# Transposes moved into the gaps of attention outputs, and one rounding moved behind a copy

## The chip, the cores and the metric

The kernel runs on one core of one Trainium2 chip. The core has TensorE (PE; its weight loads are shown apart as PEld), VectorE (DVE), ScalarE (ACT), GpSimd (POOL) and SyncE (SP, which here only issues DMAs). Each engine works through its own queue in the order in which the program was written; they meet at semaphores. The metric is the device time of one execution in microseconds (us).

## The reference

Retention (linear attention with decay, no softmax) feeds a two-layer network. B = 8 batches, H = 8 heads, S = 576 positions, 64 numbers per head; 4608 tokens in all, 512 numbers each; the hidden layer has 2048.

```python
scores = scale * np.matmul(q, k.transpose(0, 1, 3, 2))
gamma = 1.0 - 2.0 ** (-5.0 - np.arange(H, dtype=np.float32))
Dmat = np.where(rel >= 0, gamma[:, None, None] ** rel[None, :, :], 0.0)
ret = scores * Dmat[None, :, :, :]
out = np.matmul(ret, v)          # -> x: 4608 tokens x 512
h = x @ w_in
g = h * np.cos(h)
return (g @ w_out).astype(np.float32)
```

`rel` is the distance from a key's position to a query's.

## The kernel before, in words

**Tokens.** Attention goes by 18 blocks of 256 tokens, numbered from 0; the network goes by 9 tiles of 512 tokens, so tile n takes blocks 2n and 2n + 1. The decay is split into a factor on q and one on k, so that a masked product of chunks and a running state of 64 x 64 per head replace the full matrix: what a chunk gets from its own tokens goes through masked scores, and what it gets from earlier ones through the state, which is summed in float32 (`s_all`) and rounded to bf16 (`sb`).

**What a block goes through.** Its q, k, v are loaded by SP into `fq`, `fk`, `fv`. `scaled` (L192) multiplies q and k by the decay factors into `qks`, one instruction for each half (y = 0, 1) of q and of k, on POOL or DVE. `round_v` (L210) makes `vb`. `turned` (L225) transposes all of `qks` on TensorE with 32 small matmuls into PSUM, and two copies (`evacs`, L245) bring it to `qkT`; with two banks named, each copy has a bank of its own tag, and with one bank both halves lie in one PSUM tile. `scores` (L281) and `sums_of` (L347) are 32 and up to 32 small matmuls; DVE masks the scores into `ret` (L337) and adds the states (L406, L410), ACT rounds them (L420). `outputs` (L488) computes the block's result: `out_own` (L430) in two halves of 16 or 32 small matmuls, `out_carried` (L467) from the rounded states, and an ACT copy into the network's input x (L492).

**Between the halves of `out_own`.** The two halves write the same PSUM places from different rows of the array, so the second must wait until the first is complete. Without a guard, TensorE drains. With a guard, ACT makes a tiny copy (`flag`, L461) that waits for the first half, the second half waits for that copy, and the guard's instructions fill the time between: held-back ACT copies of outputs, and TensorE work such as the next block's states and scores.

```python
            if swap and guard is None:
                nc.tensor.drain()
            elif swap:
                gate = nc.scalar.copy(flag[:, 1:], flag[:, :1])
```

**The network.** `mm1` (L505) is the first matmul of one tile: 64 matmuls of 128 x 512 in 8 blocks (tiles 0 and 1 go in halves of 256 columns), in three PSUM buffers in turn; ACT takes the cosine and DVE multiplies (L530, L531). Work of the attention can be put inside it (`inside`, L950). `fillers` (L93) spreads a number of no-operations through a tile's `mm1`. The second matmul is direct for tile 0 (L1015, with an ordered list of steps, `todo`, put in between), and by `mm2_seven` (L648) with seven products of half size for tiles 1 to 8. It needs sums of blocks of g on DVE and POOL (L569) and sums of weights (L549). Between the products, `at` names which step of the attention goes where; results are copied by ACT (`held`, L660), added by DVE (L656, put off in `pend` until `flush`) and stored by SP. All the order is written out by hand.

**The places that matter here.** In tile 0's second matmul: block 2's outputs at step 58, the turn of block 3 at step 63, then the rounding of its v on ACT. In tile 1: after the last product but one, `last_outputs` (L1081) makes block 5's outputs. In tile 2: `mm1` has the turn of block 6 in its second block and that of block 7 in its sixth (L957, L958). Its products go in the order 1, 2, 6, 4, 7, 5, 3. Before product 2 comes `turning` (L1033) with block 8's turn; before 6 `only_intro` (L1048) with states and scores of block 6; before 7 `mid_unit` (L1085) with block 6's outputs, whose guard does the states and scores of block 7; before 3 `end_unit` (L1098) with block 7's outputs, whose guard does those of block 8. From tile 3 on the pattern is the same in each tile.

Of the kernel before, what the change touches and what calls it, by code (L numbers as in the profile page):

```python
# [17 lines left out]
def kernel(  # L18
# [9 lines left out]
    nc = tc.nc  # L28
# [4 lines left out]
    HP = P // 2  # L33
# [56 lines left out]
    w_in_sb = consts.tile([P, DG, DF], BF16)  # L90
    w_out_sb = consts.tile([P, ET, DM], BF16)

    fillers = {1: 80, 2: 76, 3: 126, 4: 48, 5: 64, 6: 64, 7: 128}  # L93
    tiles = {}

    class Chunk:
# [125 lines left out]
    def new_qkT(j):  # L222
        tiles["qkT", j] = nat.tile([P, 2, 2, HG, P], BF16, tag="qkT", name="qkT")

    def turned(j, banks, evacs=(nc.scalar.copy,) * 2):  # L225

        new_qkT(j)
        shape = [P, 2, 2, HG, HP]
        if len(banks) == 1:
            both = psum.tile([P, 2, *shape[1:]], BF16, tag=banks[0], name="tr")  # L230
            pss = [both[:, r] for r in range(2)]
        else:
            pss = [psum.tile(shape, BF16, tag=t, name="tr") for t in banks]
        for m in range(2):
            for y in range(2):
                for hg in range(HG):
                    for r in range(2):
                        rows = slice(r * HP, r * HP + HP)
                        nc.tensor.transpose(  # L239
                            pss[r][:, m, y, hg, :],  # L240
                            tiles["qks", j][rows, m, y, hg].rearrange("s a d -> s (a d)"),
                            ident[rows, rows],
                        )
        for r in range(2):
            evacs[r](tiles["qkT", j][:, :, :, :, r * HP : r * HP + HP], pss[r])  # L245

    def transpose_pe(j, name, bank, evac, ys=(0, 1)):
        if ("qkT", j) not in tiles:
# [181 lines left out]
    def out_own(j, ps, guard=None):  # L430

        ret = tiles["ret", j]
        vb = tiles["vb", j]
        begun = set()
        gate = None
        if chunks[j][0].pair:
            order = [(c, y) for c in chunks[j] for y in range(2)]
        else:
            order = [(c, c.y) for c in chunks[j]]
        for swap in (1, 0):  # L440
            for hg in range(0, HG, 2):
                for c, y in order:
                    he = c.half ^ swap
                    for h in (head(he, hg), head(he, hg + 1)):
                        part = (h % 2, he)
                        i = nc.tensor.matmul(  # L446
                            ov_cols(c, ps, h, c.n),
                            lhsT=vb[c.rows, y, h, :],
                            rhs=ret[c.rows, he, h % HG, y, :],
                            start=part not in begun,  # L450
                            stop=False,
                            skip_group_check=True,
                        )
                        if gate is not None:
                            after(i, gate)
                            gate = None
                        begun.add(part)
# [4 lines that stand above are left out]
                after(gate, i)  # L462
                while held:
                    held.pop(0)()
                guard()

    def out_carried(j, ps):  # L467
        cs = [c for c in chunks[j] if c.carry]
# [13 lines left out]
    def x_of(j):  # L482
        n = j // 2
        if ("x", n) not in tiles:
            tiles["x", n] = xp.tile([P, DG, W], BF16, tag="xT", name="xT")
        return tiles["x", n][:, :, j % 2 * BK : j % 2 * BK + BK]

    def outputs(j, bank, guard=None):  # L488
        ps = psum.tile([P, DG, BK], F32, tag=bank, name="ov")
        out_own(j, ps, guard)  # L490
        out_carried(j, ps)
        nc.scalar.copy(x_of(j), ps)  # L492

    def spread(n, w):

# [441 lines left out]
    def states_and_scores(j, st_bank, sc_bank):  # L937
# [4 lines left out]
        for masked in masks:  # L942
            masked()

    stores = []

    for n in range(NT):
        blocks = blocks_of.get(n) or [(e + k * E2, 0, W) for e in range(0, E2, 2) for k in range(2)]
        for i, (et, c0, cw) in enumerate(blocks):
            inside = {  # L950
                (0, 0): {2: block1_own, 3: block1_carried},
                (1, 0): {3: lambda: states_and_scores(3, None, ("n", "st"))},
                (1, 1): {3: lambda: adds.append(sums_of(3, ("n", "st"))())},
                (1, 2): {3: lambda: (adds.pop()(), w_sums(4, 4, E2))},
                (1, 4): {2: lambda: turned(4, ("st", "a"), (act, vec))},
                (1, 7): {2: lambda: turned(5, "m")},
                (2, 1): {1: lambda: turned(6, ("n", "st"))},  # L957
                (2, 5): {1: lambda: turned(7, ("n", "st"))},  # L958
            }.get((n, i), {})
            mm1(n, et, c0, cw, banks_of.get(n, turn_of(n) * 3)[i], inside)  # L960
            if (n, i) == (1, 0):
                step(False)
                load_next()
            if (n, i) == (1, 1):
                step(False)
                for r0, ot in stores[3:] + stores[:3]:
                    stored_rows(r0, 0, DM, ot)
                load_next()
                step()
            if (n, i) == (1, 3):  # L970
                w_sums(7, 0, 4)
                w_sums(7, 4, E2)
                mm2_seven(1, {}, None, (1,), lambda: outputs(3, "a"))
            if n:
                sums_after(n, i)
            if n == 2 and i in (2, 4):
                for y in range(2):
                    scaled(nc.gpsimd, 8, "q" if i == 2 else "k", y)
            if (n, i) == (2, 6):
                round_v(8)  # L980
                prepared = 9
                load_next()
                load_next()
        if n == 0:
# [6 lines left out]
                (36, lambda: turned(2, "ab", (act, vec))),  # L991
                (36, lambda: round_v(2)),
                (45, lambda: states_and_scores(2, "a", "b")),
                (46, lambda: prep(3, nc.vector)),
                (60, load_next),
                (63, lambda: turned(3, "ab", (act, vec))),
                (63, lambda: round_v(3, (act, act))),
                (58, lambda: outputs(2, "b")),
            ]
            todo += [  # L1000
                (at, lambda x=x, e=e: w_sums(x, e, e + 4))
# [29 lines left out]
        sc_bank, out_bank, st_bank = turn_of(n)  # L1031

        def turning(flush, pend):  # L1033
            for j, bank in ((b, st_bank), (b + 1, sc_bank)) if n > 2 else ((8, "m"),):
                if j < NB:
                    turned(j, bank)

        def first_unit(flush, pend):
            visit(b, sc_bank, st_bank, pend, flush, (a, out_bank))
# [7 lines left out]

        def only_intro(flush, pend):  # L1048
            flush()
            add = sums_of(a, "a")  # L1050
            for masked in scores(a, "m"):
                masked()
            add()()
# [25 lines left out]
            pass  # L1079

        def last_outputs(flush, pend):  # L1081
            outputs(b, "a")
            flush()

        def mid_unit(flush, pend):  # L1085
            masks, sums = [], []

            def middle():
                sums.append(sums_of(b, "b"))
                masks.extend(scores(b, "m"))  # L1090

            outputs(a, "a", middle)
            for masked in masks:
                masked()
            flush()
            sums[0]()()

        def end_unit(flush, pend):  # L1098
            visit(b + 1, "a", "b", pend, flush, (b, "m"))
# [47 lines left out]
```

## Time and profile before

| what | us |
|---|---|
| median of 3 runs | 294.38 |
| lowest, highest | 294.01, 295.45 |
| the profiled execution | 294.59 |
| its span, first to last instruction | 292.9 |

The profile is of one execution. Its span is divided among engines: a row of a timeline has the start, the time from the first start to the last end of what was merged into it, the engine, the line of the kernel, the operation, the tiles written and read, the count, and in brackets the idle time before it and what ended that. Ends of matmuls are modelled and overlap with what follows; starts, and above all the starts of weight loads, tell when TensorE came to something. A few matmul records can be missing.

### The profile page before, as it was taken

To read this page: it belongs to the slowest core of one execution; us is meant where nothing else is said; L and a number is where in the kernel's file an instruction comes from. 1 tells how busy PE (TensorE), PEld (TensorE's weight loads), DVE (VectorE), ACT (ScalarE), POOL (GpSimd) and SP (SyncE) were. 2 spreads that over 40 slices of the span, in tenths; PEclk is the share of its full clock that TensorE was granted. 3 is DMA by queue.
4 is the path that set the end of the run, shared out by engine and by line. 5 is a ranking of instruction groups with operands and counts; after the bars stand their busy time and mean duration, and the time that the engine had idled before them with its cause. 6 is when DMAs were issued, how large, how long until landed. Compare 5 with 4: busy or idle time off the path is not lost.

```text
span 292.9 us, 10506 instructions
## 1 busy us (share of the span) xinstructions
PE 283.8 (97%) x4365; PEld 195.7 (67%) x4385; DVE 218.6 (75%) x308; ACT 171.2 (58%) x201; POOL 143.4 (49%) x165
## 2 busy tenths in 40 slices
PE   8899999999999999999999999999999999999994
PEld 3578546888754786468746874688458845884584
DVE  5766747889948896897779776986698669745943
ACT  4766317756568745677476736673767476535620
POOL 7931353578595993369235933494248014101410
PEclk9999999999999999999999999999999999999999
DMA  7999999788997996915881489229201220112013
GB/s 226 263 184 204 249 243 249 188 202 214 236 243 200 258 257 167 223 32 119 208 214 41 101 208 222 50 63 249 58 0 40 55 57 0 40 47 64 0 38 107
DMA packets 103837, 42.62 MB, mean 146 GB/s; under 512 B 68464, under 2 KB 103280, under 8 KB 103792
## 3 DMA queue, kind: packets, MB, share of 16 engines
q1 hardware_dynamic: 99104, 37.37, 52.5%
q0 software_dynamic: 4240, 4.19, 8.9%
q8 instruction: 36, 0.59, 0.8%
q10 hardware_dynamic: 448, 0.39, 0.4%
q14 instruction: 9, 0.07, 0.1%
HBM read 36.70 MB, written 9.44 MB: 158 GB/s over the span
## 4 chain that ended last, share of the span: by engine, by line
PE 89%; DVE 6%; issue 2%; DMA 1%; ACT 1%; DVEq 0%
PE h L519 42%; PE o L630 31%; PE o L1015 5%; PE tr L239 3%; PE ov L446 3%; PE ov L473 2%; PE sc L328 2%; DVE ret L308 1%; DMA fk<-in_k_dram 1%; PE st L361 1%; DVE qks L171 1%; DVE gs L569 1%; DVE ret L337 1%; DVE s_all L410 1%; DVE gT L531 0%
## 5 line engine op out<-in xcount | busy, mean ns | idle before, releaser
L519 PE MATMUL h<-xT,w_in_sb 128*128 128x512 bf16 (+1 forms) x689 | 126.9, 340 | 1.0 <-issue 0.2
L531 DVE TENSOR_TENSOR gT<-h,cosh 128x1024 bf16<-128x1024 f32 x72 | 87.6, 1222 | 29.0 <-ACT cosh L530 28.7
L519 PEld LDWEIGHTS <-w_in_sb 128*128 128x128 bf16 x704 | 68.1, 98 | 54.6 <-issue 0.5
L530 ACT ACTIVATE cosh<-h,half_pi 128x1024 f32<-128x1024 f32 x72 | 79.8, 1114 | 39.5 <-PE h L519 39.4
L569 POOL TENSOR_TENSOR gs<-gT 128x512 bf16<-128x512 bf16 x28 | 35.8, 1278 | 99.6 <-DVE gT L531 99.6
L630 PEld LDWEIGHTS <-gs 128*128 128x128 bf16 x528 | 49.4, 98 | 6.3 <-DVE gs L569 0.4
L630 PEld LDWEIGHTS <-gT 128*128 128x128 bf16 x384 | 36.6, 98 | 6.1
L203 POOL TENSOR_TENSOR qks<-fk,gkc 128x512 bf16<-128x512 f32 x32 | 37.6, 1192 | 5.3 <-DMA fk<-in_k_dram 5.2
L656 DVE TENSOR_TENSOR ot<-ot,o 128x512 f32<-128x512 f32 x35 | 23.2, 683 | 21.5 <-ACT ot L660 14.2
L203 POOL TENSOR_TENSOR qks<-fq,gq 128x512 bf16<-128x512 f32 x29 | 32.6, 1144 | 12.5 <-DMA fq<-in_q_dram 12.5
L245 ACT COPY qkT<-tr 128x1024 bf16<-128x1024 bf16 x29 | 27.7, 1021 | 10.1 <-PE tr L239 10.1
L630 PE MATMUL o<-w_out_sb,gs 128*128 128x256 bf16 (+1 forms) x264 | 30.8, 270 | 0.1
L630 PE MATMUL o<-w_out_sb,gT 128*128 128x256 bf16 x256 | 30.6, 273 | 0.0
L630 PE MATMUL o<-ws,gs 128*128 128x256 bf16 (+1 forms) x264 | 30.5, 270 | 0.0
L660 ACT COPY ot<-o 128x512 f32<-128x512 f32 x33 | 19.2, 585 | 15.3 <-PE o L630 15.3
L420 ACT CAST sb<-s_all 128x768 bf16<-128x768 f32 (+2 forms) x17 | 15.7, 921 | 20.9 <-DVE s_all L410 17.8
L337 DVE TENSOR_TENSOR ret<-sc,mask_c 128x512 bf16<-128x512 f32 x32 | 20.6, 684 | 5.6 <-PE sc L328 4.5
L492 ACT CAST xT<-ov 128x1024 bf16<-128x1024 f32 x16 | 16.2, 1012 | 10.6 <-PE ov L473 10.5
L410 DVE TENSOR_TENSOR s_all<-st,s_all 128x256 f32<-128x256 f32 x49 | 20.7, 422 | 1.3
L214 POOL CAST vb<-fv 128x512 bf16<-128x512 f32 x33 | 20.5, 647 | 1.2 <-DMA fv<-in_v_dram 1.0
L569 DVE TENSOR_TENSOR gs<-gT 128x512 bf16<-128x512 bf16 (+1 forms) x25 | 17.5, 700 | 0.5
L630 PE MATMUL o<-ws,gT 128*128 128x256 bf16 x128 | 15.3, 273 | 0.0
(82 smaller groups left out, 212.7 us busy)
## 6 DMA issues: line engine op xcount, KB each, us to landing
out_dram<-ot SPq DMA_DIRECT2D x68, 128.0 KB, 2.5
fk<-in_k_dram SPq DMA_DIRECT2D x28, 256.0 KB, 5.1
fv<-in_v_dram SPq DMA_DIRECT2D x28, 256.0 KB, 4.9
fq<-in_q_dram SPq DMA_DIRECT2D x12, 512.0 KB, 5.0
w_out_sb<-in_moe_w_out_dram POOLq DMA_DIRECT2D x4, 512.0 KB, 10.1
w_in_sb<-in_moe_w_in_dram POOLq DMA_DIRECT2D x3, 512.0 KB, 8.5
fq<-in_q_dram SPq DMA_DIRECT2D x4, 384.0 KB, 5.8
fk<-in_k_dram SPq DMA_DIRECT2D x2, 512.0 KB, 4.9
```

The source lines that it names most:

```text
L203: return eng.tensor_tensor(out=dst.rearrange("p b a d -> p a b d"), in0=src.rearrange("p (a b) d -> p a b d", a=2), in1=by.rearrange("p (a ...
L214: runs[y](vb[:, y], f[:, :, y, :] if j < NP_B else f[:, y])
L245: evacs[r](tiles["qkT", j][:, :, :, :, r * HP : r * HP + HP], pss[r])
L337: nc.vector.tensor_tensor(out=ret[:, he].rearrange("p b y i -> p (b y) i"), in0=ps[he].rearrange("p b y i -> p (b y) i"), in1=mask_c.unsqu ...
L410: nc.vector.tensor_tensor(out=s32[:, u], in0=ps[c.half][:, c.y], in1=s32[:, u - 1] if u else tiles["run"], op=ALU.add,)
L519: nc.tensor.matmul(ps[:, j, :], lhsT=w_in_sb[:, dg, (et + j) * P : (et + j + 1) * P], rhs=xT[:, dg, c0 : c0 + w], start=dg == 0 and not (i ...
L530: nc.scalar.activation(cosh, ps, ACTF.Sin, bias=half_pi, scale=1.0)
L531: nc.vector.tensor_mul(gT[:, et : et + m, c0 : c0 + w], ps, cosh)
L569: i = eng.tensor_tensor(out=tiles["gs", n, x][:, e : e + step], in0=a[:, e : e + step], in1=b[:, e : e + step], op=op_,)
L630: nc.tensor.matmul(dst[i], lhsT=lhs[:, e, j * P : (j + 1) * P], rhs=rhs[:, e, c0:c1], start=(fresh and e == 0 and (i == 0 or len(parts) > 2)),
L656: return lambda: nc.vector.tensor_tensor(out=out_, in0=in0, in1=in1, op=ALU.add)
L660: held.append(lambda ps=tiles["all", x]: nc.scalar.copy(t, ps))
```

## The change

- Tile 0: the turn of block 3 becomes the guard of block 2's outputs, so that its drain is gone and a gate is there instead. The transposes of k come first (`ms=(1, 0)`), both halves lie in the one bank "a", and the two copies out (ACT and DVE) are issued after the copy of x (`later`). Of the scaling of block 3's q, one half goes to POOL (`prep3`); before, DVE did both.
- Tile 1: the turn of block 6 leaves tile 2's `mm1` and becomes the guard of block 5's outputs, in bank "m", copied out by ACT and DVE; this drain is gone too. The DVE copy is issued ahead of the additions of `flush`.
- Tile 2: the turn of block 7 leaves `mm1` and follows that of block 8 before product 2, in bank "a". Of each turn's two copies one goes to DVE; ACT did both of block 8's before. The states of block 6 go to bank "b" instead of "a".
- Tile 2: the rounding of block 7's states is put off from the end of `mid_unit` to the next `flush`, which comes behind product 7's output copy on ACT.
- Tile 2 has 80 fillers instead of 76.

```diff
-    fillers = {1: 80, 2: 76, 3: 126, 4: 48, 5: 64, 6: 64, 7: 128}
+    fillers = {1: 80, 2: 80, 3: 126, 4: 48, 5: 64, 6: 64, 7: 128}
...
-    def turned(j, banks, evacs=(nc.scalar.copy,) * 2):
+    def turned(j, banks, evacs=(nc.scalar.copy,) * 2, ms=(0, 1), later=False):
...
-        for m in range(2):
+        for m in ms:
...
-        for r in range(2):
-            evacs[r](tiles["qkT", j][:, :, :, :, r * HP : r * HP + HP], pss[r])
+        runs = [
+            lambda r=r: evacs[r](tiles["qkT", j][:, :, :, :, r * HP : r * HP + HP], pss[r])
+            for r in range(2)
+        ]
+        if later:
+            return runs
+        for run in runs:
+            run()
...
-                guard()
+                rest = guard()
+        return rest or ()
...
-        out_own(j, ps, guard)
+        rest = out_own(j, ps, guard)
         out_carried(j, ps)
         nc.scalar.copy(x_of(j), ps)
+        for run in rest:
+            run()
...
+    def prep3():
+        for name, y in (("k", 0), ("k", 1), ("q", 0)):
+            scaled(nc.gpsimd, 3, name, y)
+        scaled(nc.vector, 3, "q", 1)
...
-                (2, 1): {1: lambda: turned(6, ("n", "st"))},
-                (2, 5): {1: lambda: turned(7, ("n", "st"))},
...
-                (46, lambda: prep(3, nc.vector)),
+                (46, prep3),
                 (60, load_next),
-                (63, lambda: turned(3, "ab", (act, vec))),
+                (58, lambda: outputs(2, "b", lambda: turned(3, "a", (act, vec), (1, 0), True))),
                 (63, lambda: round_v(3, (act, act))),
-                (58, lambda: outputs(2, "b")),
...
-            for j, bank in ((b, st_bank), (b + 1, sc_bank)) if n > 2 else ((8, "m"),):
+            for j, bank in ((b, st_bank), (b + 1, sc_bank)) if n > 2 else ((8, "m"), (7, "a")):
                 if j < NB:
-                    turned(j, bank)
+                    turned(j, bank, (act, vec if n == 2 else act))
...
-            add = sums_of(a, "a")
+            add = sums_of(a, "b")
...
-            outputs(b, "a")
+            outputs(b, "a", lambda: turned(6, "m", (act, vec), later=True))
...
-            sums[0]()()
+            pend.append(sums[0]())
```

## The prediction

> **What bounds the kernel now.** I read the page's busy times first, then the chain of waits, then a table of two stages, then the timeline of each place that the diff touches, one engine at a time.
>
> ```profile
> PE 283.8 (97%) x4365; PEld 195.7 (67%) x4385; DVE 218.6 (75%) x308; ACT 171.2 (58%) x201; POOL 143.4 (49%) x165
> ```
>
> TensorE is busy nearly throughout, and the chain that ended last is PE for 89% and DVE for 6%. So time is won only where TensorE gets less to do or waits less, and lost where another engine comes late for it. Stage table of the first matmul of token tiles 2 and 3 (columns: stretch, length, busy time and count by engine, clock, DMA share, GB/s):
>
> ```profile
> 82.06:97.25 15.19, 14.93 (x127) 7.13 (x128) 9.75 (x10) 11.23 (x11) 11.24 (x12) 1.00 0.96 232
> 113.84:127.66 13.82, 13.71 (x65) 6.26 (x65) 11.39 (x15) 8.52 (x8) 3.85 (x3) 1.00 0.71 167
> ```
>
> Both hold the same 64 matmuls; tile 2 has two turns of 32 transposes inside. Its excess of 1.37 us is the price of two free-standing turns, 0.68 each. The clock is 1.00 in both.
>
> Weight loads at the outputs of block 5 (its halves parted by a drain) and of block 8 (a guard of 64 small matmuls between the halves):
>
> ```profile
> 79.37 0.21 PEld L446 LDWEIGHTS <-vb 64*64 64x64 bf16 x16 [0.43 <-DVE ret L337]
> 79.79 0.21 PEld L446 LDWEIGHTS <-vb 64*64 64x64 bf16 x16 [0.21 <-issue]
> ```
>
> ```profile
> 134.14 0.21 PEld L446 LDWEIGHTS <-vb 64*64 64x64 bf16 x16 [0.21 <-issue]
> 134.26 0.35 PEld L361 LDWEIGHTS <-qks 64*64 64x64 bf16 x32
> 134.53 0.36 PEld L328 LDWEIGHTS <-qkT 64*64 64x64 bf16 x32
> 134.80 0.36 PEld L446 LDWEIGHTS <-vb 64*64 64x64 bf16 x16
> ```
>
> From the first half to the second it is 0.42 with the drain and 0.66 with the guard. A half issues in 0.12 (134.14 to 134.26).
>
> The vector and scalar queues in the second matmul of tile 2, up to the gate of block 6's outputs:
>
> ```profile
> 98.60 1.22 DVE L531 TENSOR_TENSOR gT<-h,cosh 128x1024 bf16<-128x1024 f32 x1
> 99.86 0.68 DVE L569 TENSOR_TENSOR gs<-gT 128x512 bf16<-128x512 bf16 x1
> 100.57 0.98 DVE L569 TENSOR_TENSOR gs<-gs,gT 128x1024 bf16<-128x1024 bf16 x1
> 101.68 0.69 DVE L656 TENSOR_TENSOR ot<-ot,o 128x512 f32<-128x512 f32 x1
> 102.30 1.29 DVE L337 TENSOR_TENSOR ret<-sc,mask_c 128x512 bf16<-128x512 f32 x2
> 103.50 0.87 DVE L410 TENSOR_TENSOR s_all<-st,s_all 128x256 f32<-128x256 f32 x2
> 104.29 0.42 DVE L406 COPY s_all<-st 128x256 f32<-128x256 f32 x1
> ```
>
> ```profile
> 104.74 0.83 ACT L420 CAST sb<-s_all 128x768 bf16<-128x768 f32 x1 [3.04 <-DVE s_all L406]
> 105.48 0.58 ACT L660 COPY ot<-o 128x512 f32<-128x512 f32 x1
> 106.12 0.19 ACT L461 COPY flag<-flag 128x1 f32<-128x1 f32 x1
> ```
>
> DVE has no gap above 0.13 in this stretch; the rounding waits 3.04 for its last addition, the copy of an output and the gate (flag) stand behind the rounding in ACT's order, and the second half's loads start at 106.41. They are 0.67 behind the first half's (105.74), as in the undisturbed case above. So this chain and TensorE now arrive together: its slack is nil.
>
> The same queue at block 7's outputs, whose halves start at 110.50 and 111.54:
>
> ```profile
> 109.71 1.04 ACT L420 CAST sb<-s_all 128x1024 bf16<-128x1024 f32 x1 [1.53 <-DVE s_all L410]
> 110.66 0.58 ACT L660 COPY ot<-o 128x512 f32<-128x512 f32 x1
> 111.14 0.19 ACT L461 COPY flag<-flag 128x1 f32<-128x1 f32 x1
> ```
>
> Here the halves are 1.04 apart: the gate stands behind rounding and copy, and TensorE loses 1.04 - 0.66 = 0.38.
>
> **The change part by part.** One price first. Sixty-four transposes at 129.50 issue in 0.99, so 32 take 0.50; of a free-standing turn's 0.68 that leaves 0.18, or 0.09 for each change between large and small operands. As a guard, a turn makes the halves 0.12 + 0.09 + 0.50 + 0.09 = 0.80 apart, against 0.42 with the drain: +0.38. No row shows transposes between two halves. The low end is +0.24 (the gate's 0.66, if switching costs nothing); the high end takes each switch at the drain's 0.30 (0.42 - 0.12): 1.22, +0.80. I take 0.38, since the 0.09 comes from transposes.
>
> (a) Block 3's turn into block 2's outputs: -0.68 + 0.38 = -0.30 for TensorE. But the turn is moved before five 512-column matmuls, and its q rows are ready late. The outputs start at 45.68, the 16 k transposes end at 45.68 + 0.12 + 0.09 + 0.25 = 46.14. The q load is issued at 38.02 and takes 6.8 to land, 44.8. From there POOL scales one half and DVE (free from 45.09) the other. The pair like it:
>
> ```profile
> 37.58 1.55 POOL L203 TENSOR_TENSOR qks<-fq,gq 128x512 bf16<-128x512 f32 x1 [3.04 <-DMA fq<-in_q_dram]
> ```
>
> DVE ran its half beside it (37.53, 0.69), and both together took 1.60 instead of POOL's usual 1.04. So both halves are there at about 46.5 and TensorE waits 0.27 to 0.39, by which half is the late one; I take 0.33. The scalar queue then does x (from about 47.4), the turn's copy and the output's copy, 1.01 + 1.02 + 0.59 less some overlap, and frees bank n at about 49.95, where block 3's scores want it (49.95 now): 0.05. Sum for (a) +0.08; ends -0.30 (no wait) and +0.54 (dear switches and nothing else gained). Before, DVE finished q at 46.37 for transposes at 47.73, so there were 1.36 of cover; they are gone. POOL's added half falls into its idle time (44.55 to 49.62). The sums of weights on DVE slip by one copy of 0.69 and are not awaited before 49. SP's order of loads is unchanged.
>
> (b) Block 6's turn into block 5's outputs: +0.38 (0.24 to 0.80) there. Its q and k are ready by 70.5. DVE's copy now stands ahead of the closing additions at 79.34 and waits for the transposes until about 80.3, so the last of them ends near 84.5 instead of 82.95; SP reaches those stores only at 84.65 and DVE's next product is due at 85.25, so this is hidden, by 0.2 and 0.7.
>
> (c) Tile 2's first matmul loses both turns: -1.37. The ACT copies go with them; POOL's scaling of block 8 must be done 15.7 after the stage's start, and now ends 16.2 after it, paced in part by the same products, which come earlier; I count no wait, at most 0.3.
>
> (d) Blocks 8 and 7 turned together: 64 transposes take 129.50 to 130.54, 1.04, where 32 take 99.09 to 99.67, 0.58: +0.46.
>
> (e) Of their four copies two go to DVE, in front of the addition, masks and states of block 6: 2 x 0.69 = +1.38 in the chain shown above that has no slack. TensorE itself is 0.46 later, so the gate makes it wait 0.92. ACT keeps two copies, as now. Low end 0 (cover that I don't see), high end 1.38.
>
> (f) Block 7's rounding behind the copy: that copy waits only for a product that ends at 108.6, so it is done at about 109.4 to 110.0 and the gate no longer queues behind it; the rounding ends about 110.75 plus any shift, before the carried part needs it: -0.38, at worst 0. The additions on DVE that waited 1.60 for that copy come earlier, off the path.
>
> The four more fillers cost nothing that I can see: tile 3 has 126 in a stage without excess.
>
> Sum: 0.08 + 0.38 - 1.37 + 0.46 + 0.92 - 0.38 = +0.09 us. The profiled execution took 294.59 (span 292.9 and 1.7 around it), so it would be 294.68; the median shown is 294.38, 0.21 lower, and the forecast is 294.5.
>
> The Trainium skill, page TensorEngine Tiling, section Tiling Modes, Key Properties, says that changing the tiling mode, and not only the tile, drains TensorE. It speaks against (a) and (b), which put 64-row by 128-column work between 64 by 64 halves four times over; the 0.09 agrees with a cheap drain. With each switch as dear as the explicit drain the sum would be +0.93, which is the rival R2 below.
>
> **The rivals.**
>
> R1, the vector queue does not carry (e). Against it: the queue is dense and the gate is already just on time. For it: products and sums of tile 2 may come earlier than I shift them once ACT's turn copies are out of the first matmul. Then the sum is 0.09 - 0.92 = -0.83, or 293.6, and with no wait in (a) 293.2.
>
> R2, the other side, dear switches: (a) and (b) each 0.42 more, +0.93, 295.3. It decides from 0.10 a switch upward: each further 0.1 adds 0.4 over the four. For it: the 0.30 of the drain at 79.79; against it: 0.09 beside large matmuls.
>
> R3, block 3's q lands late: the cover of 1.36 is gone, so each us of lateness is one of TensorE's. Loads of these tiles in the stretch 25 to 60 take 4.5 to 8.2 by the medians of their groups; at 8.2 instead of 6.8 the sum is +1.5, 296.0. It decides from the first tenth; against it is that the order of loads is the same.
>
> R4, the reordered rounding does not help, because the gate still comes late: +0.47, 294.9.
>
> **How the numbers follow.** The forecast holds with 0.46 (with R4 inside it), 294.0 to 295.0; R1 0.25, R2 0.11, R3 0.08; 0.10 for what no row shows, shared by both sides. The range goes from R1's better case with a little scatter to R3: 293.1 to 296.0. A measurement of this kernel tells about 0.5%, 1.47 us, from no change. Below 292.9 only R1's better case with scatter and the unseen reach, 0.15; above 295.85, R3, the upper part of R2 and the unseen, 0.18; the rest, 0.67, is within.
>
> **What would show it.** Halves of blocks 2 and 5's outputs 0.8 apart, block 2's with a wait on qks in the middle; 13.8 in tile 2's first matmul; 1.0 for 64 transposes after its first product; two DVE copies of 0.69 ahead of L656, then block 6's halves 1.6 apart instead of 0.67; block 7's halves 0.66 apart. I am wrong if the gate at block 6 is on time (R1), if the halves are over 1 us apart without a wait on qks (R2), or if a later stage, which the change does not touch, has another length.

## The result, and the profile after

| | before | after |
|---|---|---|
| median, us (4 runs each) | 294.28 | 297.11 |
| lowest, highest | 294.01, 295.45 | 296.31, 299.94 |
| profiled execution | 294.59 | 299.94 |
| its span | 292.9 | 298.2 |
| mean granted clock in it | 1.000 | 0.992 |

The change makes the kernel slower: the ratio is 1.011, 95% interval 1.0084 to 1.0137. The profiled execution of after is the longest of its four; the other three took 297.07, 296.31 and 297.14 at a clock of 0.999 or more, so some of what this profile shows is its own, and it is told apart below. Ratios, here and below, leave out executions more than 1.5% above the shortest of the same kernel.

The totals on the page of after:

```profile
PE 285.6 (96%) x4366; PEld 197.5 (66%) x4385; DVE 218.9 (73%) x310; ACT 169.4 (57%) x200; POOL 144.6 (48%) x166
PEclk9999999799999999999999999999999999999999
```

TensorE is busy 1.8 longer than before, with the same work. One slice of the 40, the eighth (52.2 to 59.6), has a lower clock. So the place to look is tile 0's end, not tile 2, where I had most of my terms.

The span of after falls into these pieces (starts of the same weight loads in both traces):

| stretch of TensorE's work | before | after | difference |
|---|---|---|---|
| start to the first half of block 2's outputs | 45.68 | 45.83 | +0.15 |
| from there to the scores of block 3 | 4.27 | 7.73 | +3.46 |
| from there to block 4's turn | 10.29 | 11.82 | +1.53 |
| to block 5's outputs (first half) | 19.13 | 18.74 | -0.39 |
| block 5's outputs up to tile 2's first matmul | 2.69 | 3.09 | +0.40 |
| tile 2's first matmul | 15.19 | 13.81 | -1.38 |
| its second matmul | 16.59 | 18.15 | +1.56 |
| from tile 3 on | 179.06 | 179.03 | -0.03 |

All but 0.3 of the difference of 5.3 lies in the second and third row. The four rows of tiles 1 and 2 (the fourth to the seventh) sum to +0.19; my terms (b) to (f), which lie there, gave +0.01.

What happens in the second row, in the timeline of after (start, time, engine, line, operation, tiles, count, idle before it and what ended that):

```profile
45.83 0.21 PEld L452 LDWEIGHTS <-vb 64*64 64x64 bf16 x16 [0.42 <-issue]
46.08 0.29 PEld L239 LDWEIGHTS <-qks 64*128 64x128 bf16 x16
46.22 0.69 DVE L203 TENSOR_TENSOR qks<-fq,gq 128x512 bf16<-128x512 f32 x1 [0.90 <-DMA fq<-in_q_dram]
46.27 1.55 POOL L203 TENSOR_TENSOR qks<-fq,gq 128x512 bf16<-128x512 f32 x1 [1.24 <-DMA fq<-in_q_dram]
47.87 0.29 PEld L239 LDWEIGHTS <-qks 64*128 64x128 bf16 x16 [1.50 <-POOL qks L203]
48.21 0.21 PEld L452 LDWEIGHTS <-vb 64*64 64x64 bf16 x16
...
48.81 1.01 ACT L499 CAST xT<-ov 128x1024 bf16<-128x1024 f32 x1 [2.35 <-PE ov L480]
49.72 1.02 ACT L245 COPY qkT<-tr 128x1024 bf16<-128x1024 bf16 x1
50.77 0.69 DVE L245 COPY qkT<-tr 128x1024 bf16<-128x1024 bf16 x1 [3.25 <-ACT qkT L245]
51.36 0.11 PEld L334 LDWEIGHTS <-qkT 64*64 64x64 bf16 x2 [0.21 <-ACT ot L1036]
51.38 1.53 DVE L558 TENSOR_TENSOR ws<-w_out_sb,ws 128x1024 bf16<-128x1024 bf16 x1
52.84 0.68 DVE L1036 COPY ot<-o 128x512 f32<-128x512 f32 x1
53.56 0.44 PE L334 MATMUL sc<-qkT 64*64 64x64 bf16 x31 [1.99 <-DVE ot L1036]
```

There are two waits of TensorE here. The first is on q of block 3. Its load landed so late that DVE began its half at 46.22 and POOL at 46.27; POOL's took 1.55 beside DVE's and ended at 47.82, and the 16 transposes of q go at 47.87. The halves of the outputs are 2.38 apart (45.83 to 48.21), 1.58 more than the 0.80 that I took for a turn without a wait.

The second wait I had not seen at all. The DVE copy of the turn waits 3.25 for the ACT copy of the same turn, though it needs only transposes that were done at about 48.3. Both copies read one PSUM tile now, and they run one after the other. The ACT copy stands behind the cast of x in ACT's order, and the DVE copy behind the ACT copy; behind the DVE copy stand in DVE's order a sum of weights (1.53; before, it ran ahead of the copy, at 46.89) and the copy of tile 0's last output, and that output's PSUM bank is where the scores of block 3 want to go. TensorE comes to them at 51.36, and they start in earnest at 53.56: 2.20. Part of this is the sum: it took 1.53 here, where the part alone, below, has 0.68 for it, and that 0.85 is about the whole difference between 2.20 and the wait of 1.36 there.

The two waits and the guard's gain add up: -0.30 + 1.58 + 2.20 = 3.48, against 3.46 measured.

The third row of the table is the clock. Two stretches of the first matmul of tile 1 in after (columns: stretch, length, busy time and count of PE, PEld, DVE, ACT and POOL, granted clock, DMA share, GB/s):

```profile
54.00:57.00 3.00, 3.00 (x26) 2.00 (x28) 2.50 (x3) 1.11 (x1) 1.92 (x3) 0.59 1.00 252
57.00:60.00 3.00, 3.00 (x53) 2.61 (x54) 2.16 (x6) 1.59 (x2) 2.03 (x3) 0.84 0.95 214
```

PE is busy all the time, and the clock is 0.59 and then 0.84. That costs 3 x 0.41 + 3 x 0.16 = 1.7, about the 1.53 of the table, and it follows right on the two waits. The Trainium skill, page TensorE: Matmul & The Clock Gate, Part 1, says that the clock is halved after an idle window of some 3.4 us that runs by itself. The trace does not show that rule: neither wait is that long (1.58 and 2.20), and TensorE works for 3.5 between them (47.87 to 51.36). That the waits brought the clock down is not shown either. Executions with a mean clock of 0.994 came up in the kernel before (297.59), with tile 0's part undone (296.28) and with copies on ACT and no-operations moved (294.88), kernels whose profiles have neither wait; these three executions themselves were not profiled.

Tile 2, by the weight loads of after (the outputs of block 5 first):

```profile
84.12 0.21 PEld L452 LDWEIGHTS <-vb 64*64 64x64 bf16 x16 [0.35 <-DVE ret L343]
84.36 0.52 PEld L239 LDWEIGHTS <-qks 64*128 64x128 bf16 x32
84.94 0.21 PEld L452 LDWEIGHTS <-vb 64*64 64x64 bf16 x16
...
102.86 0.99 PEld L239 LDWEIGHTS <-qks 64*128 64x128 bf16 x64 [0.21 <-issue]
...
106.30 0.30 PEld L334 LDWEIGHTS <-qkT 64*64 64x64 bf16 x28 [0.21 <-issue]
107.59 0.11 PEld L334 LDWEIGHTS <-qkT 64*64 64x64 bf16 x3 [0.98 <-issue]
...
111.33 0.21 PEld L452 LDWEIGHTS <-vb 64*64 64x64 bf16 x16 [0.21 <-issue]
...
112.00 0.23 PEld L452 LDWEIGHTS <-vb 64*64 64x64 bf16 x16
...
116.22 0.21 PEld L452 LDWEIGHTS <-vb 64*64 64x64 bf16 x16 [0.21 <-DVE ot L665]
...
116.90 0.21 PEld L452 LDWEIGHTS <-vb 64*64 64x64 bf16 x16
```

Block 5's halves are 0.82 apart, block 6's 0.67 and block 7's 0.68. The wait that I had put at block 6's gate is not there. In its place stands a stop of about 1.0 in the middle of block 6's scores, between two loads of the same tile, that no engine ended ("issue").

### The profile page after: what moved, and what is told of

Its sections match the earlier page's. It is cut to its first block, busy times and chain, and to the rows that moved or that the text cites. A ratio compares the mean times of both kernels' runs of the same rounds, so it can differ in the third digit from the quotient of the medians.

```text
span 298.2 us, 10510 instructions
## 1 busy us (share of the span) xinstructions
PE 285.6 (96%) x4366; PEld 197.5 (66%) x4385; DVE 218.9 (73%) x310; ACT 169.4 (57%) x200; POOL 144.6 (48%) x166
## 4 chain that ended last, share of the span: by engine, by line
PE 72%; DMA 10%; DVE 7%; POOL 3%; SPq 2%; ACT 2%; issue 1%; POOLq 0%
PE h L528 34%; PE o L639 29%; DMA fq<-in_q_dram 5%; DMA w_in_sb<-in_moe_w_in_dram 3%; PE tr L239 2%; PE ov L452 2%; DVE gs L578 2%; DVE gT L540 2%; DMA fv<-in_v_dram 2%; SPq L140 2%; PE sc L334 1%; PE ov L480 1%; POOL qks L203 1%; ACT cosh L539 1%; PE st L367 1%
## 5 line engine op out<-in xcount | busy, mean ns | idle before, releaser
L528 PEld LDWEIGHTS <-w_in_sb 128*128 128x128 bf16 x704 | 68.9, 99 | 55.6 <-issue 0.3
L203 POOL TENSOR_TENSOR qks<-fq,gq 128x512 bf16<-128x512 f32 x30 | 35.1, 1189 | 9.3 <-DMA fq<-in_q_dram 8.6
L203 POOL TENSOR_TENSOR qks<-fk,gkc 128x512 bf16<-128x512 f32 x32 | 36.9, 1173 | 5.3 <-DMA fk<-in_k_dram 5.2
L245 ACT COPY qkT<-tr 128x1024 bf16<-128x1024 bf16 x26 | 24.9, 1023 | 9.5 <-PE tr L239 9.5
L214 POOL CAST vb<-fv 128x512 bf16<-128x512 f32 x33 | 19.9, 629 | 1.1 <-DMA fv<-in_v_dram 1.1
```

What stands on the lines that cost most here:

```text
L203: return eng.tensor_tensor(out=dst.rearrange("p b a d -> p a b d"), in0=src.rearrange("p (a b) d -> p a b d", a=2), in1=by.rearrange("p (a ...
L214: runs[y](vb[:, y], f[:, :, y, :] if j < NP_B else f[:, y])
L245: lambda r=r: evacs[r](tiles["qkT", j][:, :, :, :, r * HP : r * HP + HP], pss[r])
L528: nc.tensor.matmul(ps[:, j, :], lhsT=w_in_sb[:, dg, (et + j) * P : (et + j + 1) * P], rhs=xT[:, dg, c0 : c0 + w], start=dg == 0 and not (i ...
```

## The experiments

The theory after the result, call it T: the loss is all in (a), the block 3 edit, by the two waits; and the second wait comes from the one PSUM tile with two readers. Rivals: the loss is in tile 2 and only shows earlier; or it is the late q alone (R3 of the prediction); or it is the switches of tiling (R2). Inside tile 2 the question was what the stop in block 6's scores is: the DVE copies of (e), or something of TensorE's own. Before was run beside every group; where its median is given, it is that group's.

**Tile 0's part undone.** Tile 2 keeps all of the change.

```diff
-                (46, prep3),
+                (46, lambda: prep(3, nc.vector)),
-                (58, lambda: outputs(2, "b", lambda: turned(3, "a", (act, vec), (1, 0), True))),
+                (63, lambda: turned(3, "ab", (act, vec))),
+                (58, lambda: outputs(2, "b")),
-    fillers = {1: 80, 2: 80, ...
+    fillers = {1: 80, 2: 78, ...
```

> The changed kernel with tile 0's part undone (block 3's turn back at step 63 in banks a and b, block 2's outputs with their drain, both halves of q on DVE; 78 fillers in tile 2). Theory T (the loss is in tile 0: TensorE waits 1.57 us for block 3's q inside the guard and 2.2 us at block 3's scores): parts (b) to (f) are worth +0.2 us in the profile after, so this one takes 294.0 to 295.0 us and is the same as before within 0.3%; the scores of block 3 follow 1.4 us after the start of tile 1's first matmul. Rival S (the loss is in tiles 1 and 2, and the profiled execution's waits in tile 0 are its own): it stays above 296 us. Either way the wait of about 1.07 us inside block 6's scores stays.

Measured: 294.44 (293.63 to 296.28, 10 runs) against 294.54 before; ratio 1.0000, interval 0.9983 to 1.0018. The whole loss is gone. From block 2's outputs to block 3's scores it takes 4.26, as before. So T's place is right, and the rival that puts the loss in tile 2 is out, since (b) to (f) together are worth nothing that can be measured: +0.0 with an interval of 0.5 either way.

**Tile 0's part alone**, in the kernel before (with 78 fillers in tile 2).

```diff
-                (46, lambda: prep(3, nc.vector)),
+                (46, prep3),
-                (63, lambda: turned(3, "ab", (act, vec))),
+                (58, lambda: outputs(2, "b", lambda: turned(3, "a", (act, vec), (1, 0), True))),
-                (58, lambda: outputs(2, "b")),
```

> The kernel before with tile 0's part of the change alone (78 fillers in tile 2). Theory T: 296.3 to 297.5 us, and block 3's scores are held by 1.5 to 2.3 us behind DVE's copy of an output, which stands behind the turn's DVE copy, which waits for ACT's copy of the same PSUM tile. Rival S: 294.2 to 294.8 us.

Measured: 296.70 (296.02 to 298.17, 5 runs); ratio 1.0078, interval 1.0052 to 1.0104. In the timeline of this kernel:

```profile
48.12 1.02 ACT L245 COPY qkT<-tr 128x1024 bf16<-128x1024 bf16 x1
...
49.17 0.69 DVE L245 COPY qkT<-tr 128x1024 bf16<-128x1024 bf16 x1 [2.24 <-ACT qkT L245]
49.78 0.68 DVE L558 TENSOR_TENSOR ws<-w_out_sb,ws 128x1024 bf16<-128x1024 bf16 x1
...
51.12 0.44 PE L334 MATMUL sc<-qkT 64*64 64x64 bf16 x31 [1.14 <-DVE ot L1038]
```

In this execution, the shortest of the five, q came nearly in time: the halves are 45.65 and 46.61, 0.96 apart, a wait of 0.16. The second wait is there all the same, 1.36 (49.76 to 51.12). The stretch from outputs to scores takes 5.47, +1.20; the terms give -0.30 + 0.16 + 1.36 = 1.22. So the second wait does not need the first, and it is the one that is paid in both profiles with this part as the change has it.

**Both copies of block 3's turn on DVE**, in after.

```diff
-                (58, lambda: outputs(2, "b", lambda: turned(3, "a", (act, vec), (1, 0), True))),
+                (58, lambda: outputs(2, "b", lambda: turned(3, "a", (vec, vec), (1, 0), True))),
```

> The changed kernel with both copies of block 3's turn on DVE. Theory T1 (of tile 0's loss the larger part is the copies' order: the DVE copy waits for ACT's, ACT's stands behind the copy of x): DVE copies right after the transposes, the wait of 2.2 us at block 3's scores shrinks to 0.3 or less and the time falls by about 2 us, to 294.5 to 295.3. Rival Q (the late q carries it and the wait at the scores only follows from it): the wait at the scores shrinks little and the time stays at 296.3 or more.

Measured: median 295.24, spread from 293.61 to 299.77 in 10 runs; ratio 1.0003, interval 0.9981 to 1.0026. The two longest, 299.07 and 299.77, had mean clocks of 0.992 and 0.993; the other eight have a median of 294.87. In the timeline of one of the eight (297.02, clock 1.000):

```profile
48.43 0.41 PE L239 MATMUL tr<-ident,qks 64*128 64x64 bf16 x16 [1.76 <-POOL qks L203]
...
48.88 1.29 DVE L245 COPY qkT<-tr 128x1024 bf16<-128x1024 bf16 x2 [0.81 <-PE tr L239]
...
50.52 1.47 PE L528 MATMUL h<-xT,w_in_sb 128*128 128x256 bf16 x12
...
51.92 0.45 PE L334 MATMUL sc<-qkT 64*64 64x64 bf16 x32
```

The copies follow the transposes at once, and the scores follow the twelve matmuls with no wait: the second wait is gone. The first is 1.96 here (halves 46.01 and 48.77), and the stretch takes 5.91, +1.64; the terms give -0.30 + 1.96 = 1.66. So both waits are real, each without the other. By these medians the second carries most of the loss: without it the kernel takes 294.87 instead of 297.11, 2.2 of the 2.8 that the change costs.

No run set the landing of q by itself, but the profiles show that it changes without any edit near it. In the kernels whose tile 0 is that of before, or differs only after q is scaled, the first scaling of q on DVE starts at 45.06 to 45.28 in seven profiles, where DVE comes free, and at 45.68, 46.07, 46.12 and 46.34 in four, waiting for the load. One of the four in the timeline, of tile 0's part undone:

```profile
46.07 1.29 DVE L203 TENSOR_TENSOR qks<-fq,gq 128x512 bf16<-128x512 f32 x2 [0.75 <-DMA fq<-in_q_dram]
```

And of a kernel described below, which differs from it in its no-operations alone:

```profile
46.34 1.29 DVE L203 TENSOR_TENSOR qks<-fq,gq 128x512 bf16<-128x512 f32 x2 [0.81 <-DMA fq<-in_q_dram]
```

There the transposes of q come at about 47.9 and the lateness is hidden. Where the turn is a guard, DVE started its half at 45.06 (part alone), 46.22 (after) and 46.78 (both copies on DVE), and TensorE waited 0.16, 1.58 and 1.96. That this also makes the wide spread of the times is an inference.

**One bank for block 3's turn, nothing else**, in the kernel before.

```diff
-                (63, lambda: turned(3, "ab", (act, vec))),
+                (63, lambda: turned(3, "a", (act, vec))),
```

> The kernel before, with block 3's turn left at step 63 but in one bank (a) with one copy on ACT and one on DVE, as in the change. If two copies out of one PSUM tile go one after the other across the engines, DVE's starts at the end of ACT's, about 49.4 us instead of 48.45, the output's copy behind it ends near 50.8 and block 3's scores start 0.7 to 1.0 us later: 295.0 to 295.5 us. If the order of the copies does not matter, both start together and the time is that of before.

Measured: 295.42 (295.24 to 296.82, 10 runs) against 294.71; ratio 1.0020, interval 0.9990 to 1.0051, which by itself is not told from no change. Its timeline tells more:

```profile
48.37 1.01 ACT L245 COPY qkT<-tr 128x1024 bf16<-128x1024 bf16 x1 [0.21 <-PE tr L239]
49.42 0.69 DVE L245 COPY qkT<-tr 128x1024 bf16<-128x1024 bf16 x1 [0.80 <-ACT qkT L245]
50.02 0.68 DVE L1025 COPY ot<-o 128x512 f32<-128x512 f32 x1
...
50.76 0.44 PE L328 MATMUL sc<-qkT 64*64 64x64 bf16 x31 [0.65 <-DVE ot L1025]
```

In the kernel before, with two banks, the two copies run side by side:

```profile
48.41 1.01 ACT L245 COPY qkT<-tr 128x1024 bf16<-128x1024 bf16 x1 [0.21 <-PE tr L239]
48.45 0.69 DVE L245 COPY qkT<-tr 128x1024 bf16<-128x1024 bf16 x1 [0.88 <-PE tr L239]
```

With one bank DVE's starts when ACT's is done. The scores start 5.12 after block 2's outputs instead of 4.27: +0.85. So sharing a bank is enough to put the copies in order, and through DVE's queue it reaches TensorE. What it costs in the change is more, because there the ACT copy itself stands behind the cast of x. No run gave the guard's turn two banks, so what the change would take with them is not shown.

With these, the stretch from block 2's outputs to block 3's scores, and the same terms for each kernel (the guard's -0.30 only where the turn is a guard):

| kernel | stretch | over before | wait on q | wait at the scores | sum of terms |
|---|---|---|---|---|---|
| before | 4.27 | | | | |
| tile 0's part undone | 4.26 | -0.01 | 0 | 0 | 0 |
| one bank only | 5.12 | +0.85 | 0 | 0.87 | 0.87 |
| both copies on DVE | 5.91 | +1.64 | 1.96 | 0 | 1.66 |
| tile 0's part alone | 5.47 | +1.20 | 0.16 | 1.36 | 1.22 |
| after | 7.73 | +3.46 | 1.58 | 2.20 | 3.48 |

From the scores to block 4's turn it is 10.28 or 10.29 in all but after, where the clock fell.

**The stop in tile 2.** In the profile of the kernel with tile 0's part undone, the stop is again in block 6's scores, 0.61 long:

```profile
102.13 0.11 PEld L334 LDWEIGHTS <-qkT 64*64 64x64 bf16 x2 [0.50 <-issue]
```

The next four kernels start from that one and ask whether it hangs on the DVE copies of turns 8 and 7, or on the place in TensorE's instruction stream. Forty of tile 3's no-operations moved into tile 2's first matmul shift that place and take nothing else away.

Only the no-operations moved:

```diff
-    fillers = {1: 80, 2: 78, 3: 126, ...
+    fillers = {1: 80, 2: 118, 3: 86, ...
```

> The kernel a_undone with 40 of tile 3's fillers moved to tile 2 and nothing else. Theory F (the stop inside block 6's scores is TensorE's instruction stream reaching a new block too early): the stop is gone, and the DVE copies, no longer covered by it, hold the gate of block 6: its halves 1.1 to 1.3 us apart instead of 0.67. Theory D alone (the DVE copies cause the stop): the stop of 0.6 to 1.1 us stays where it is.

Measured: 294.72 (293.54 to 296.15, 10 runs) against 294.71; ratio 0.9997, interval 0.9968 to 1.0025. Its weight loads:

```profile
105.99 0.21 PEld L452 LDWEIGHTS <-vb 64*64 64x64 bf16 x16 [0.21 <-issue]
...
107.19 0.14 PEld L334 LDWEIGHTS <-qkT 64*64 64x64 bf16 x6 [0.49 <-issue]
107.23 0.23 PEld L452 LDWEIGHTS <-vb 64*64 64x64 bf16 x16
```

The stop has left block 6's scores and now stands in block 7's, inside block 6's guard. That fits a place in the stream, and not block 6's scores or what they wait for; but each is one profile, and the stops turn out below to come and go. The halves of block 6 are 1.24 apart, and the gate (106.73) was late as well, so the second half would have waited even without the stop.

Both copies of turns 8 and 7 on ACT instead of one each on DVE, no-operations not moved:

```diff
-                    turned(j, bank, (act, vec if n == 2 else act))
+                    turned(j, bank, (act, act))
```

> The kernel a_undone with both copies of blocks 8 and 7's turns on ACT and the fillers left. Theory D: the stop inside block 6's scores goes, the time from the start of tile 2's second matmul to that of tile 3's first falls from 17.67 to about 16.8 us. Theory F: a stop of 0.5 to 1.1 us stays in the last scores of block 6, at the same instruction, ending 2.4 us after an instruction transfer starts, and the stretch stays at 17.4 us or more.

Measured: 294.45 (293.66 to 295.91, 10 runs) against 294.71; ratio 0.9989, interval 0.9960 to 1.0018. Both edits:

> The kernel a_undone with both copies of blocks 8 and 7's turns on ACT and 40 of tile 3's fillers moved to tile 2 (118 and 86). It takes away both suspected causes of the 1.4 us that tile 2's second matmul still loses: the two DVE copies (theory D), and the place at which TensorE's instruction stream passes from one 16 KB block to the next (theory F: in the profiles the unexplained stops of TensorE, in before at block 7's outputs and in after at block 6's scores, lie exactly 512 instructions apart and both end 2.4 to 2.5 us after an instruction transfer began). Both expect the 1.07 us wait inside block 6's scores to be gone and the gate of block 6 on time, 293.0 to 293.7 us; if neither is the cause it stays, and the time equals a_undone's.

Measured: 294.22 (293.35 to 295.92, 10 runs) against 294.54; ratio 0.9991, interval 0.9974 to 1.0009.

The second matmul of tile 2 in four kernels (columns as above): before, tile 0's part undone, and copies on ACT.

```profile
97.25:113.84 16.59, 16.37 (x441) 14.07 (x440) 14.52 (x23) 9.25 (x13) 15.27 (x17) 1.00 0.97 237
```

```profile
96.03:113.70 17.67, 17.18 (x474) 14.74 (x473) 16.47 (x27) 9.46 (x13) 15.75 (x17) 1.00 0.95 227
```

```profile
95.94:112.60 16.66, 16.66 (x474) 14.47 (x473) 15.54 (x24) 11.30 (x15) 15.76 (x17) 1.00 0.96 232
```

With the copies on DVE this stage is 17.67 long, with both on ACT 16.66; with both edits it is 16.76 (95.85 to 112.61). In the last two profiles no stop is to be seen. The 1.0 in these single profiles does not come back in the medians, 294.44 against 294.45 and 294.22.

The rounding of block 7's states put back ahead of the copy, with both other edits:

```diff
-            pend.append(sums[0]())
+            sums[0]()()
```

> The kernel u_actact_shift with the rounding of block 7's states back in its old place. If the rounding in front of the copy held the gate (the reading on record), block 7's halves are 0.9 to 1.05 us apart instead of 0.67, the time is 0.25 to 0.4 us longer. If the stop of 0.41 us in the kernel before was the instruction stream alone, the halves stay at 0.67 to 0.75 us.

Measured: 294.04 (293.31 to 295.06, 10 runs) against 294.71; ratio 0.9975, interval 0.9950 to 0.9999. Leaving (f) out does not make it slower; if anything the other way. Its weight loads at block 7's outputs:

```profile
109.94 0.21 PEld L452 LDWEIGHTS <-vb 64*64 64x64 bf16 x16 [0.21 <-issue]
...
110.82 0.21 PEld L452 LDWEIGHTS <-vb 64*64 64x64 bf16 x16
```

0.88 apart, against 0.68 in after: the gate is late again, by 0.2.

The version with copies on ACT and no-operations moved, once more with more runs, as the likeliest to beat before:

> The kernel u_actact_shift once more, timed longer: the changed kernel without tile 0's part, both copies of both turns on ACT, 40 fillers moved from tile 3 to tile 2. By its profile tile 2 is 1.2 us shorter than before; if the time follows, 293.0 to 293.8 us and a ratio of 0.995 to 0.998; if the time is taken back elsewhere, 294.0 to 294.6.

Measured: 294.07 (293.37 to 296.08, 12 runs) against 294.58 (17 runs); ratio 0.9992, interval 0.9972 to 1.0011. The nearest to a gain is the kernel with the rounding put back, whose interval ends at 0.9999; no version was clearly shown to beat the kernel before.

**Three kernels profiled again**, to see whether the stop stays where it was.

> The kernel a_undone, a second execution to look at. If the stop inside block 6's scores hangs on when the instruction transfer gets through, its length differs from 0.61 us and it again ends 2.4 us after the start of that transfer, or is absent where the transfer starts under 1.5 us after the last passing of a block; if it is set by the DVE copies it has 0.6 us again and ends with a DVE instruction. The gate of block 6 is late by the DVE copies only as far as the stop has not covered them.

> The kernel u_actact, a second execution. Its first had no stop, and its instruction transfer had started 0.96 us after the last passing of a block. If that was chance, a stop of up to 1 us may appear here at the same instruction; if the DVE copies are the cause, there is none, and block 6's halves are 0.67 apart again.

> The kernel before, a second execution. If the 0.41 us stop at block 7's outputs was the gate behind rounding and copy, the halves are 0.85 to 1.05 us apart again; the part of it that the instruction stream made can be absent, and then the halves are 0.85 to 0.9 apart, as in u_round.

Measured: 294.72, 294.59 and 294.36. Weight loads of the first of them, tile 0's part undone:

```profile
105.84 0.21 PEld L452 LDWEIGHTS <-vb 64*64 64x64 bf16 x16 [0.21 <-issue]
...
106.81 0.21 PEld L452 LDWEIGHTS <-vb 64*64 64x64 bf16 x16 [0.22 <-ACT flag L467]
```

Now there is no stop in block 6's scores, and block 6's gate is late, as the prediction had it: the halves are 0.97 apart, 0.3 over the 0.67 of an undisturbed gate. In the second, with copies on ACT, there are stops where its first profile had none:

```profile
101.91 0.11 PEld L334 LDWEIGHTS <-qkT 64*64 64x64 bf16 x2 [0.47 <-issue]
...
106.73 0.11 PEld L452 LDWEIGHTS <-vb 64*64 64x64 bf16 x2 [0.20 <-issue]
```

And in the third, the kernel before:

```profile
110.33 0.21 PEld L446 LDWEIGHTS <-vb 64*64 64x64 bf16 x16 [0.21 <-issue]
...
111.21 0.21 PEld L446 LDWEIGHTS <-vb 64*64 64x64 bf16 x16 [0.17 <-ACT flag L461]
```

Block 7's halves are 0.88 apart here, where the first profile of before had 1.04. That first profile has, between the two halves, the row

```profile
111.53 0.11 PEld L328 LDWEIGHTS <-qkT 64*64 64x64 bf16 x2 [0.33 <-issue]
```

which the second does not have: a stop of the same kind, in the kernel before too. So these stops come and go between executions of one kernel, and one profile cannot price an edit to better than about 1 us here.

## Why the prediction was wrong

The forecast was 294.5, within 0.5%; measured is 297.11, beyond the range's high end of 296.0. The step that failed is (a), "Sum for (a) +0.08; ends -0.30 (no wait) and +0.54": the stretch cost +3.46 in the profile, and the executions of the part alone ran about 2.2 over before.

- **The late q (in (a)).** I took a wait of 0.33, from a load of 6.8 and a landing at 44.8. It came some 1.4 later in after's profile, where the load was issued 0.5 later (38.52 for 38.02) and took about 7.7, and the wait was 1.58. The mechanism was in the prediction, as R3: "the cover of 1.36 is gone, so each us of lateness is one of TensorE's". What was wrong is its size and its chance. The step put a single load time of before into a place where TensorE now waits for it, and gave a chance of 0.08 to the case that it was late (at 296.0, where a load of 8.2 makes its sum 295.9), with "the order of loads is the same" against it. The order was the same and the time was not: q was late in four of eleven profiles where it costs nothing, and in two of three where it does.
- **The scores of block 3 (in (a)).** I gave 0.05, by following ACT's queue and bank n. I wrote that the sums of weights on DVE "slip by one copy of 0.69 and are not awaited before 49", and did not ask when that copy could start. It could start only after ACT's copy, because both now read one PSUM tile; that moved the whole DVE queue, with it the copy of the last output, and with that the bank for the scores: 2.20 in after (0.85 of it the longer sum), 1.36 in the part alone, 0.87 from the one bank by itself. The diff shows it ("ab" to "a"), and the description of the change says that both halves lie in one bank; I treated the bank as a name and not as an order.
- **The clock** was 1.00 in all that I read, and I had no term for it. In after's profile it took 1.53. No other profile here shows it, and its cause is open.
- **(b)** held in time: halves of block 5 0.82 apart, predicted 0.80. It missed the same order of copies as (a): out of the one tile of block 6's turn, DVE's copy waited 3.50 for ACT's and started at 87.57 in after. The closing additions behind it ended at 90.91, 6.8 after block 5's outputs, where I had 5.1 (84.5 less 79.37). That is more than the room of 0.2 and 0.7 that I had counted, and yet TensorE waited for none of it, with tile 2's first matmul at 13.81: there the forecast had luck. The 0.82 also settles R2: a switch costs about 0.1 there, not 0.30, and 32 transposes between two 64 by 64 halves ran at the pace of the free-standing ones.
- **(c)** held: 13.81 for tile 2's first matmul, predicted 13.8; -1.38 against -1.37.
- **(d)** held: 64 transposes from 102.86 take 1.04 to the next work (103.90), predicted 1.04.
- **(e)** had the right mechanism with too large a size, and was not always what ended the wait. By starts of matmuls, from the stage's start to block 6's second half it took 9.18 in before (97.25 to 106.43), 10.23 in the second profile of tile 0's part undone (96.59 to 106.82) and 9.64 with the copies on ACT. Against before that is +0.46 with the copies on ACT, which is (d) to the digit, and +1.05 with two of them on DVE; so the copies cost 0.59, where I had 0.92. DVE's queue is as dense as I read it: the rounding behind it starts 8.77 into the stage instead of 7.49, later by what the two copies take one after the other (1.27 from 101.13, where I had 1.38). But the gate starts only 1.11 later (9.98 instead of 8.87). So the chain had about 0.2 of slack ahead of the gate, which I had put at nil. In after the gate was in time, because a stop in the stream had held TensorE back by as much.
- **(f)** was 0.2 and not 0.38. Of the 1.04 that I read between block 7's halves, 0.16 was a stop of the kind told above that the second profile of before does not have. The remaining 0.88 went to 0.68 with the change and came back as 0.88 with the rounding put back. In the time it could not be seen (0.9975 without it, 0.9991 with).
- **R1** (no carry of (e)) looks right in after's own gate, 0.67 apart, but the second profile of tile 0's part undone shows the carry. **R4** is refuted by the 0.68.

For tiles 1 and 2 the sum came out near zero, as forecast, but partly by compensation: (e) and (f) were each smaller than I had them, and the stops make up the rest in a given profile.

## What to carry to other kernels

When a PSUM tile is shared by two copies on two engines, follow the second engine's queue from the moment at which the first copy can start, and price everything that stands behind the second copy; in tile 1 the same order cost nothing, and in tile 0 it cost most of the loss. When work is moved ahead of something that covered a load, read the spread of that load's landing over executions and not one value, since from then on TensorE pays for the late cases. Where a place is priced from one profile, look for rows in which TensorE stops with no engine to blame, and take a second profile before dividing tenths among edits.

## What the runs showed of the hardware

TensorE stops at places that lie a fixed number of instructions apart. If its weight loads, matmuls, no-operations, drains and semaphore instructions are counted from the start (a matmul for each weight load), the stops come at count 3777 (before, at 111.53; the part alone, 112.67), 3265 (after, 107.59; tile 0's part undone, 102.13; copies on ACT, second profile, 101.91; both copies on DVE, 104.44) and 3521 (no-operations moved, 107.19; copies on ACT, second profile, 106.73). From the weight load before to the one after they take 0.31 to 1.10. These counts are 256 apart, and each stop ends 2.3 to 2.5 after a transfer of 16 KB on the instruction queue began (for example 105.12 to 107.59 and 99.72 to 102.13). Over all 14 profiles TensorE passes these three counts 42 times, and never earlier than 2.18 after the start of the last transfer. So TensorE seems to have run out of fetched instructions in this dense stretch, where 256 of them pass in about 4.5 (101.91 to 106.73, less the stop). Moving 40 no-operations ahead of the place moved the stop, which fits; no run changed the transfers themselves, so the cause is argued and not isolated. The Trainium skill, page Runtime: NRT & Kernel Launch, section Instruction fetch mechanics, has the same blocks of 16 KiB or 256 instructions and calls the cost of crossing one mostly hidden; here it was hidden in some executions, and if this is that cost, it took from 0.31 to 1.10 in others.

Two instructions that multiply or add from SBUF, one on DVE and one on POOL at the same time, do not both keep their usual time here, and in the four pairs that I compared it is the one that began second that is longer. Block 3's q in after: DVE from 46.22 takes 0.69, POOL from 46.27 takes 1.55 instead of 1.04. In the part alone POOL began first: POOL from 44.74 takes 1.04, DVE from 45.06 takes 1.27. The sum of weights in after, from 51.38, takes 1.53 beside a scaling on POOL from 51.32 that takes 1.04; in the part alone the sum, from 49.78, takes 0.68, and POOL's scaling from 49.96 takes 1.40. So with a late load the split of q over two engines did not help: POOL's half set the wait and ended at 47.82, 0.9 after DVE's. DVE alone takes 1.29 for both halves, which from 46.22 gives 47.5, an estimate.
